# Attention: where the split of the queries stands, who clears the value tiles, and when the first weights are loaded

## The chip, the core and the metric

The kernel runs on one core of a Trainium2 chip as one program. The core has five engines, each with a queue of its own that runs in order: TensorE (PE in the rows) for matrix products, VectorE (DVE), ScalarE (ACT), GpSimd (POOL), and SyncE (SP), which here only issues DMAs. They wait for each other through semaphores. The metric is the time of the whole program on the device, in microseconds; lower is better.

## The reference

Three stages follow each other. Only the first is touched by the change.

```python
# attention: q, k, v are (2, 12, 448, 64), float32
scores = (1.0 / np.sqrt(64)) * np.matmul(q, k.transpose(0, 1, 3, 2))
scores = np.where(np.triu(np.ones((448, 448), dtype=bool), k=1), -1e9, scores)
scores = scores - np.max(scores, axis=-1, keepdims=True)
attn = np.exp(scores)
attn = attn / (np.sum(attn, axis=-1, keepdims=True) + 1e-09)
x = np.matmul(attn, v)                  # to (896, 768)
# feed-forward: w_in (768, 2048), w_out (2048, 768)
h = np.maximum(x @ w_in, 0.0)
x = h * h @ w_out
# mixture of 8 experts: each token goes to the one of its largest logit,
# out[mask] = gate * (relu(x[mask] @ w1[e]) @ w2[e])
```

## The kernel before, in words

**Pairs.** The 24 heads are handled as 12 pairs of two heads (`units`, number 0 to 11), since two heads of 64 fill the 128 partitions. The 448 queries are cut into seven chunks of 64 (`c`, 0 to 6); chunk `c` meets only the first (c+1)*64 keys. One score product has on its rows 64 queries of one head and 64 of the other; the tile q2 holds the queries with zeros where the other head's rows would be, so that one product serves both heads.

**Splits.** Float32 numbers are handled as a rounded part and the rest, so that a product of two of them is three products of rounded numbers: kh with the rounded queries, kl with them, kh with the queries' rest. `s_prep` makes these: the rounded keys `kh` (VectorE, line 62), their rest `kl` (GpSimd, line 67), the rounded and scaled queries (ScalarE, line 60) and their rest (VectorE, line 202). For pair 0 the query parts are written directly into q2, half the partitions at a time. For all other pairs they are written into a staging tile `qs`, and two DMAs copy them into q2 (line 216). There are two q2 tiles (names q_109 and q_110 in the order), two `kh` and two `kl`, for pairs in turn; the zeros in q2 are written once, at the start, by GpSimd.

**One pair's way.** Scores (TensorE, line 243) in the order of chunks 2, 0, 1, 3, 6, 4, 5, into one of four PSUM tiles; the row maximum (VectorE, line 253; for pair 0 a plain reduction, line 250); the exponential with its sum (ScalarE, line 256); one over the sums (`rs`, lines 264 and 265); the normalisation (GpSimd, line 269); transposes of the probabilities (TensorE, line 287) into one of two PSUM tiles; their split (ScalarE line 60, VectorE line 67, `pt`); the product with the values (line 305), whose tiles `v` are split in the same way (`s_prep_v`) and have a middle third of zeros; and the split of the result into xhi and xlo.

**Order.** The loop over `k` (line 427) records half a pair at a time: with even `k`, chunks 6, 4, 5 of pair k/2 + 1; with odd `k`, chunks 2, 0, 1, 3 of the pair behind it, with transposes and value products of earlier pairs between them. TensorE keeps the recorded order up to `k` = 21 (`man_a`), and GpSimd keeps it in the start only (`zeros`). Everywhere else a scheduler orders the instructions of each engine by its own model, subject to data, buffers and explicit pins: `tc.issue_after(x)` keeps an instruction behind instruction x. In `s_prep` of pair u + 3 both the key rounding and the query split are pinned behind the maximum and the exponential of chunk 5 of the pair two before it. A small `V.memset` on one column (`hold`) ties a load to a place in VectorE's queue.

**Weights.** `w_load` brings one 128-row slice of w_in (768 KB of raw 8-byte words), which VectorE assembles into float32 (lines 121 to 125) and GpSimd splits. Loads of slice `f` are pinned behind the query copies of pair 6 + f; there are two raw buffers, and the conversions are pinned near the end of attention. The feed-forward products (`phase_a`) follow attention on TensorE, mixed into its last pairs.

## Time and profile before

| what | value |
|---|---|
| median of three runs | 561.88 us (560.63 to 562.13) |
| the profiled execution, its own time | 561.91 us |
| its span, first to last instruction | 560.2 us |
| mean granted TensorE clock | 0.996 of full speed |
| TensorE busy | 541.2 us (97%) |
| VectorE, ScalarE, GpSimd busy | 397.6, 288.3, 183.4 us |
| TensorE's waits, 57.5 to 98.5 us | 1.8 for copies of q, 0.4 for exponentials, 0.2 for pt |

All rows come from one execution. Attention fills roughly the first 100 us of the span. In rows of a timeline the first number is the start and the second the length of the group, both in us; then the engine, the line of the kernel, the operation, what it writes and reads, shape and count; in brackets stands the idle time of the engine just before, with what ended it. Idle time of an engine that nobody waits for costs nothing. TensorE's products overlap in the pipeline, so the lengths of neighbours add up to more than the time between their starts.

### The profile page before, as it was taken

What the parts mean: (1) busy time and instruction counts of PE and PEld (TensorE: products, weight loads), DVE (VectorE), ACT (ScalarE), POOL (GpSimd) and SP (SyncE); (2) the same over time, 40 slices, a digit from 0 to 9 for tenths busy, and PEclk for the clock granted to TensorE, in tenths of its full rate; (3) what the DMA queues carried; (4) which work ended last, traced back from release to release, by engine and by line L of the source; (5) the groups of instructions that cost most, each with busy time, mean ns of one, the idle gap of its engine ahead of it and who ended that gap; (6) DMA issues with size and microseconds to landing.
All of it is one profiled execution on the core that took longest, in us unless ns stands there. A gap on an engine that the chain in (4) does not pass through costs nothing.

```text
span 560.2 us, 9639 instructions
## 1 busy us (share of the span) xinstructions
PE 541.2 (97%) x3429; PEld 504.4 (90%) x3430; DVE 397.6 (71%) x957; ACT 288.3 (51%) x638; POOL 183.4 (33%) x229
## 2 busy tenths in 40 slices
PE   8899999999999999999999999999999999999993
PEld 5799889988999999999999989989999899999992
DVE  6888889755887977696653376896186898873641
ACT  4888778314425243424333236721286787763641
POOL 8878789926645643221000001001201301300010
PEclk9999999999999999999999999999999999999998
DMA  6657653332545555361000008503958879874310
GB/s 205 176 121 206 210 137 99 126 103 67 170 137 201 168 170 180 113 217 56 1 30 28 1 28 337 215 14 88 375 171 268 305 243 360 293 231 160 109 53 6
DMA packets 28234, 86.52 MB, mean 154 GB/s; under 512 B 2822, under 2 KB 13062, under 8 KB 28176
## 3 DMA queue, kind: packets, MB, share of 16 engines
q1 hardware_dynamic: 26640, 79.51, 44.0%
q0 software_dynamic: 1536, 6.29, 3.1%
q8 instruction: 29, 0.48, 0.3%
q14 instruction: 29, 0.24, 0.1%
HBM read 75.24 MB, written 6.29 MB: 146 GB/s over the span
## 4 chain that ended last, share of the span: by engine, by line
PE 83%; DVE 6%; ACT 4%; DMA 3%; issue 2%; POOL 1%; SPq 0%; POOLq 0%; ACTq 0%; DVEq 0%
PE yps L607 20%; PE ops L977 9%; PE pa L329 7%; PE pa L331 7%; PE pa L330 7%; PE pv L305 5%; PE s L243 4%; PE hps L878 3%; PE ops L915 3%; PE pt L287 2%; PE ops L910 2%; PE hps L896 2%; PE hps L898 2%; PE hps L897 2%; DVE ml L67 2%
## 5 line engine op out<-in xcount | busy, mean ns | idle before, releaser
L67 DVE TENSOR_TENSOR ml<-xraw,mh 128x768 fp32r<-128x768 f32 x64 | 59.7, 957 | 10.3 <-ACT mh L60 9.8
L60 ACT ACTIVATE mh<-xraw 128x768 fp32r<-128x768 f32 x64 | 52.3, 843 | 7.6 <-PE ops L910 5.8
L977 PE MATMUL ops<-mh,act 128*128 128x384 f32 x224 | 53.5, 342 | 0.0
L243 PE MATMUL s<-kh,q 128*128 128x128 f32 (+6 forms) x168 | 45.7, 318 | 3.8 <-ACT p L256 2.0
L256 ACT ACTIVATE p<-s,mn 128x192 f32<-128x192 f32 (+6 forms) x84 | 39.6, 478 | 16.5 <-DVE mn L253 11.5
L305 PE MATMUL pv<-pt,v 128*128 128x448 f32 (+7 forms) x288 | 47.0, 297 | 0.7 <-ACT pt L60 0.6
L269 POOL TENSOR_SCALAR p<-p,rs 128x192 f32<-128x192 f32 (+6 forms) x84 | 44.9, 552 | 4.9 <-DVE rs L265 4.5
L1003 POOL DMA_INDIRECT out<-osb,fsi x10 | 10.9, 1088 | 97.3 <-ACT osb L998 65.9
L125 DVE SCALAR_TENSOR_TENSOR w<-raw,w 128x768 int32<-128x768 int32 x32 | 41.7, 1304 | 0.7
L305 PEld LDWEIGHTS pv<-pt,v 128*128 128x128 f32 (+1 forms) x288 | 38.2, 163 | 2.7 <-ACT pt L60 0.8
L977 PEld LDWEIGHTS ops<-mh,act 128*128 128x128 f32 x224 | 39.3, 188 | 0.8
L1015 POOL DMA_INDIRECT xr<-ydram,fgi x10 | 10.5, 1051 | 86.2 <-DVE fsi L723 45.4
L67 DVE TENSOR_TENSOR pt<-pt 128x512 fp32r<-128x512 f32 x48 | 31.9, 682 | 9.1 <-ACT pt L60 9.0
L243 PEld LDWEIGHTS s<-kh,q 128*128 128x128 f32 x168 | 31.9, 205 | 7.0 <-ACT p L256 5.5
L67 DVE TENSOR_TENSOR hs<-h,hs 128x512 fp32r<-128x512 f32 (+1 forms) x32 | 21.8, 690 | 22.9 <-ACT hs L60 22.7
L253 DVE CUSTOM_DVE_ANT_0 s<-s,maskf 128x192 f32<-128x192 f32 (+6 forms) x77 | 32.2, 432 | 8.2 <-PE s L243 5.9
L123 DVE SCALAR_TENSOR_TENSOR w<-raw,w 128x768 int32<-128x768 int32 x32 | 37.1, 1160 | 0.7
L67 DVE TENSOR_TENSOR ml<-mraw,mh 128x768 fp32r<-128x768 f32 x32 | 29.9, 956 | 10.2 <-ACT mh L60 9.8
L335 ACT ACTIVATE relu<-pa 128x448 f32<-128x448 f32 x32 | 17.0, 538 | 34.0 <-PE pa L331 34.0
L60 ACT ACTIVATE pt<-pt 128x512 fp32r<-128x512 f32 x48 | 28.3, 599 | 7.0 <-PE pt L287 6.8
L121 DVE TENSOR_SCALAR w<-raw 128x768 int32<-128x768 int32 x32 | 22.6, 705 | 12.4 <-POOL wi3l L67 3.2
L1015 POOL DMA_INDIRECT xr<-ydram,egi x2 | 2.3, 1149 | 84.0 <-DVE esi L723 83.7
(463 smaller groups left out, 1667.1 us busy)
## 6 DMA issues: line engine op xcount, KB each, us to landing
xraw<-in_wm SPq DMA_DIRECT2D x32, 768.0 KB, 5.4
raw<-in_w_in SPq DMA_DIRECT2D x16, 768.0 KB, 4.2
raw<-in_w_out SPq DMA_DIRECT2D x16, 768.0 KB, 4.3
mraw<-in_wm SPq DMA_DIRECT2D x16, 768.0 KB, 5.0
qk<-in_qkd SPq DMA_DIRECT2D x11, 448.0 KB, 5.0
q<-qs SPq DMA_DIRECT2D x22, 224.0 KB, 3.8
v<-in_vd SPq DMA_DIRECT2D x12, 256.0 KB, 3.0
ydram<-ysb SPq DMA_DIRECT2D x7, 384.0 KB, 2.3
```

The costliest lines, as they stand in the source:

```text
L60: return A.activation(out, in_, AF.Copy, scale=scale)
L67: return eng.tensor_tensor(out=lo, in0=x, in1=hi, op=ALU.subtract)
L125: V.scalar_tensor_tensor(out=w[:, x], in0=raw[:, x, 0], scalar=29, in1=w[:, x], op0=ALU.logical_shift_right, op1=ALU.bitwise_or)
L243: T.matmul(ss, d["q2"][:, c, :, :, x].rearrange("p a b -> p (a b)"), d[y][:, :n], start=i_ == 0, stop=i_ == 2 and not first)
L256: last["exp", units.index(u), c] = A.activation(d["p"][c][:, :n], ss, AF.Exp, bias=mn, scale=1.0 if first else -1.0, accum_out=d["sm"][:, ...
L269: last["norm"] = G.tensor_scalar(out=p, in0=p, scalar1=rs[:, COL[c]:COL[c] + 1], scalar2=1.0, op0=ALU.mult, op1=ALU.mult)
L305: T.matmul(d["pv"][:, j * P:S] if h else d["pv"][0:D, j * P:S], d[x][:, j, 1:3].rearrange("p a b -> p (a b)") if h else d[x][:, j, 0], pt[ ...
L329: T.matmul(ps, wh[:, c], xhi[:, kc, gs], start=(kc == 0), stop=False)
L330: T.matmul(ps, wh[:, c], xlo[:, kc, gs], start=False, stop=False)
L331: T.matmul(ps, wl[:, c], xhi[:, kc, gs], start=False, stop=(kc == KC - 1))
L607: T.matmul(ps[t][c][:, :384], x, w[:, c * 384:(c + 1) * 384], start=(f == 0 and w is wh and x is hi), stop=(f == NF - 1 and x is lo))
L977: T.matmul(ps[c], x, ww[:, c * 384:(c + 1) * 384], start=(fc == 0 and x is hh and ww is wh), stop=(fc == 7 and x is hl))
```

## The change

Six things are altered, all in attention. (1) `qdir` goes from 1 to 2: pair 1's queries, as pair 0's, are split directly into q2, without `qs` and without copies. Its `s_prep` is recorded after pair 0's first products, and its rest is pinned behind the maximum of pair 0's chunk 3. (2) From pair 2 on the pins are separate: the rounded query copy behind the exponential of chunk 6 (instead of chunk 5, which is two exponentials later), the rest of the queries behind the maximum of chunk 5, and the key rounding behind that rest. (3) The zeros of the four value tiles are written by ScalarE as copies of a tile of zeros (`zero_v`) instead of by GpSimd. (4) The table `tri` is made later, at `k` = 5. (5) The loads of pair 1's values and pair 3's queries are held behind pair 0's maximum of chunk 3. (6) Loads of w_in are pinned behind the copies of pair 9 + f.

```diff
-    ch=(((2, 0, 1), (3,), ()), ((6,), (4, 5), ())), wn=[3, 2, 2], qh="A", qdir=1, qss=2, rpin=5, qdma="SS", kh="V",
+    ch=(((2, 0, 1), (3,), ()), ((6,), (4, 5), ())), wn=[3, 2, 2], qh="A", qdir=2, qss=2, rpin=5, qdma="SS", kh="V",
...
-        pin = last.get(("q", 6 + f)) if src is w_in else None
+        pin = last.get(("q", 9 + f)) if src is w_in else None
...
+    def zero_v(*xs):
+        for x in xs:
+            A.activation(x[:, :, 1], wz[:, 0:NB * D].rearrange("p (a b) -> p a b", b=D), AF.Copy)
...
-    def s_prep(u):
+    def s_prep(u, hi_pin=None, lo_pin=None, k_pin=None):
...
-        if i != 1:
+        if i == 0:
             round_k()
+            lo_pin = last["kh"]
...
-            copy_on(ENG[CFG["qh"]], hi, q, scale=SCALE)
-            return V.scalar_tensor_tensor(out=lo, in0=q, scalar=SCALE, in1=f32(hi), op0=ALU.mult, op1=ALU.subtract)
+            with behind(hi_pin):
+                last["hi"] = copy_on(ENG[CFG["qh"]], hi, q, scale=SCALE)
+            with behind(lo_pin):
+                last["lo"] = V.scalar_tensor_tensor(out=lo, in0=q, scalar=SCALE, in1=f32(hi), op0=ALU.mult,
+                                                    op1=ALU.subtract)
...
+        if i > 0:
+            with behind(last["lo"]), behind(k_pin):
+                round_k()
...
+    zero_v(*vz[0])
     s_prep(units[0])
+    with behind(last["hi"]):
+        zero_v(*vz[1])
...
-            with tc.issue_after(last["q"].ins):
-                load_v(units[1])
-                s_load(units[3])
+            load_v(units[1], last["max", 0, 3])
+            s_load(units[3], last["max", 0, 3])
...
-        if k == -3:
-            s_prep(units[1])
-            for x in vz[0] + vz[1]:
-                G.memset(f32(x[:, :, 1]), 0.0)
-            zero_p(1)
-            G.memset(tri, 1.0)
...
+        if k == -3:
+            s_prep(units[1], None, last["max", 0, 3])
+            zero_p(1)
+            zeros.__exit__(None, None, None)
...
-            x = (0, 3) if u < 0 else (u + 1, 5)
-            with tc.issue_after(last["max", *x].ins), tc.issue_after(last["exp", *x].ins):
-                s_prep(units[u + 3])
+            i = u + 1
+            s_prep(units[u + 3], last["exp", i, 6 if i else 3], last["max", i, 5 if i else 6], last["max", i, 5])
```

The first place is VectorE at the start, from the rest of pair 0's second head on. `mn` are the row maxima of pair 0, `rs` the sums before and after the reciprocal, `qs` and q_110 the query rests of pairs 1 and 2, `kh` the rounded keys. Before:

```order
L202 SCALAR_TENSOR_TENSOR q_109<-qk,q_109 64x7x64
L202 SCALAR_TENSOR_TENSOR qs<-qk,qs 128x448
L62 CAST kh<-qk 128x448
L250 TENSOR_REDUCE mn<-s 128x1 x4
L264 TENSOR_SCALAR rs<-sm 128x4
L265 RECIPROCAL rs<-rs 128x4
L202 SCALAR_TENSOR_TENSOR qs<-qk,qs 128x448
L250 TENSOR_REDUCE mn<-s 128x1 x2
L62 CAST kh<-qk 128x448
L250 TENSOR_REDUCE mn<-s 128x1
```

And now, in the changed kernel's line numbers:

```order
L215 SCALAR_TENSOR_TENSOR q_109<-qk,q_109 64x7x64
L263 TENSOR_REDUCE mn<-s 128x1 x4
L215 SCALAR_TENSOR_TENSOR q_110<-qk,q_110 64x7x64 x2
L62 CAST kh<-qk 128x448
L173 MEMSET v 128x1
L173 MEMSET qk 128x1
L277 TENSOR_SCALAR rs<-sm 128x4
L278 RECIPROCAL rs<-rs 128x4
L263 TENSOR_REDUCE mn<-s 128x1
L215 SCALAR_TENSOR_TENSOR qs<-qk,qs 128x448
L263 TENSOR_REDUCE mn<-s 128x1 x2
L62 CAST kh<-qk 128x448
```

The first four maxima have moved ahead of pair 1's split and key rounding, the split is two half-height instructions, and the fifth maximum stands ahead of pair 2's split instead of behind it.

The second place is the preparation of pair 6, behind the scores of pair 4: on ScalarE the query copy (`qs`) among the exponentials of chunks 6, 4 and 5 (128x448, 128x320, 128x384), before and then now:

```order
L256 ACTIVATE p_121,sm<-s,mn 128x448
L256 ACTIVATE p_119,sm<-s,mn 128x320
L60 ACTIVATE pt<-pt 128x512
L256 ACTIVATE p_120,sm<-s,mn 128x384
L60 ACTIVATE qs<-qk 128x448
```

```order
L269 ACTIVATE p_121,sm<-s,mn 128x448
L60 ACTIVATE qs<-qk 128x448
L269 ACTIVATE p_119,sm<-s,mn 128x320
L60 ACTIVATE pt<-pt 128x512
L269 ACTIVATE p_120,sm<-s,mn 128x384
```

The copy has moved ahead of two exponentials and one copy of transposed probabilities. On VectorE at the same place, from the maximum of chunk 5 on, before and then now (`ISA` is the masked maximum, two rows each):

```order
L253 ISA s,mn<-s,maskf 128x384
L253 ISA mn 128x1
L62 CAST kh<-qk 128x448
L265 RECIPROCAL rs<-rs 128x4
L253 ISA s,mn<-s,maskf 128x192
L253 ISA mn 128x1
L67 TENSOR_TENSOR pt<-pt 128x512
L253 ISA s,mn<-s,maskf 128x64
L253 ISA mn 128x1
L253 ISA s,mn<-s,maskf 128x128
L253 ISA mn 128x1
L202 SCALAR_TENSOR_TENSOR qs<-qk,qs 128x448
```

```order
L266 ISA s,mn<-s,maskf 128x384
L266 ISA mn 128x1
L215 SCALAR_TENSOR_TENSOR qs<-qk,qs 128x448
L62 CAST kh<-qk 128x448
L67 TENSOR_TENSOR pt<-pt 128x512
L266 ISA s,mn<-s,maskf 128x192
L266 ISA mn 128x1
```

The split of the queries has moved ahead of the key rounding, three maxima and one subtraction; the key rounding has moved back by one instruction.

The third place is SyncE's queue, where the first two loads of w_in stand among the query copies (`q`), queries and keys (`qk`) and values (`v`). Before, from the copies of pair 6 on, and now, from those of pair 9 on:

```order
L216 DMA q_109<-qs 64x7x128 x2
L176 DMA qk<-in_qkd 128x896
L116 DMA raw<-in_w_in 128x1536
L183 DMA v<-in_vd 128x512
L216 DMA q_110<-qs 64x7x128 x2
L176 DMA qk<-in_qkd 128x896
L116 DMA raw<-in_w_in 128x1536
```

```order
L226 DMA q_110<-qs 64x7x128 x2
L183 DMA qk<-in_qkd 128x896
L116 DMA raw<-in_w_in 128x1536
L226 DMA q_109<-qs 64x7x128 x2
L190 DMA v<-in_vd 128x512
L116 DMA raw<-in_w_in 128x1536
```

Both loads stand three pairs later.

## Rows read from the trace of the kernel before

**Rows 1.** Timeline of TensorE: the first score product of pairs 5 to 11.

```profile
43.16 0.34 PE L243 MATMUL s<-kh,q 128*128 128x192 f32 x1
...
50.72 0.34 PE L243 MATMUL s<-kh,q 128*128 128x192 f32 x1
...
59.62 0.34 PE L243 MATMUL s<-kh,q 128*128 128x192 f32 x1 [1.09 <-DMA q<-qs]
...
67.53 0.34 PE L243 MATMUL s<-kh,q 128*128 128x192 f32 x1
...
76.00 0.33 PE L243 MATMUL s<-kh,q 128*128 128x192 f32 x1 [0.67 <-DMA q<-qs]
...
83.81 0.34 PE L243 MATMUL s<-kh,q 128*128 128x192 f32 x1
...
92.03 0.33 PE L243 MATMUL s<-kh,q 128*128 128x192 f32 x1 [0.42 <-ACT p L256]
```

**Rows 2.** The chain of waits, at its longest DMA: start, us, what.

```profile
70.49 5.38 DMA q<-qs
```

**Rows 3.** Timeline of SyncE's queue: copies of pair 7, second weight load.

```profile
53.37 1.28 SPq L216 DMA_DIRECT2D q<-qs  x2
...
55.57 1.08 SPq L116 DMA_DIRECT2D raw<-in_w_in  x1
```

**Rows 4.** Timelines of VectorE and ScalarE around the preparation of pair 11.

```profile
83.50 0.39 DVE L62 CAST kh<-qk 128x448 fp32r<-128x448 f32 x1
...
85.36 0.71 DVE L202 SCALAR_TENSOR_TENSOR qs<-qk,qs 128x448 fp32r<-128x448 f32 x1
...
83.16 0.53 ACT L256 ACTIVATE p<-s,mn 128x320 f32<-128x320 f32 x1 [1.15 <-DVE mn L253]
...
84.70 0.62 ACT L60 ACTIVATE qs<-qk 128x448 fp32r<-128x448 f32 x1
```

**Rows 5.** Timeline of VectorE in the start.

```profile
7.82 1.17 DVE L250 TENSOR_REDUCE mn<-s 128x1 f32<-128x192 f32 x4
9.85 1.57 DVE L264 TENSOR_SCALAR rs<-sm 128x4 f32<-128x4 f32 x1 [0.86 <-ACT p L256]
...
12.07 0.62 DVE L250 TENSOR_REDUCE mn<-s 128x1 f32<-128x448 f32 x1
...
18.95 1.18 DVE L62 CAST kh<-qk 128x448 fp32r<-128x448 f32 x1
```

**Rows 6.** Timeline of GpSimd in the start.

```profile
4.54 1.38 POOL L67 TENSOR_TENSOR kl<-qk,kh 128x448 fp32r<-128x448 f32 x1 [0.60 <-DVE kh L62]
...
8.77 1.13 POOL L67 TENSOR_TENSOR kl<-qk,kh 128x448 fp32r<-128x448 f32 x1
9.84 1.07 POOL L453 MEMSET v<- 128x256 f32 x4
10.85 0.41 POOL L154 MEMSET p<- 128x64 f32 x4
...
18.60 1.28 POOL L67 TENSOR_TENSOR v<-v,v 128x512 fp32r<-128x512 f32 x1
```

**Rows 7.** Line 202, the query split: duration in ns, min/median/max, starts.

```profile
L202 DVE SCALAR_TENSOR_TENSOR qs<-qk,qs x11: 597/626/712, 7.0 to 85.4; 128x448 fp32r<-128x448 f32 x11
L202 DVE SCALAR_TENSOR_TENSOR q<-qk,q x2: 610/1012/1415, 4.3 to 5.0; 64x448 fp32r<-64x448 f32 x2
```

**Rows 8.** Timeline of ScalarE: the first query copy.

```profile
3.45 1.23 ACT L60 ACTIVATE q<-qk 64x448 fp32r<-64x448 f32 x2 [1.16 <-DMA qk<-in_qkd]
```

**Rows 9.** TensorE's waits, 98.5 to 131 us: us in total, times, longest.

```profile
PE pv L305 <- ACT pt L60: 0.6, 1, 0.6
...
PE pv L305 <- DVE pt L67: 0.2, 1, 0.2
```

**Rows 10.** Timeline of GpSimd: rounding of the first weights.

```profile
98.46 0.82 POOL L62 CAST wi0h<-w 128x768 fp32r<-128x768 f32 x1
```

**Rows 11.** The page's costliest groups: the normalisation, busy us, mean ns.

```profile
L269 POOL TENSOR_SCALAR p<-p,rs 128x192 f32<-128x192 f32 (+6 forms) x84 | 44.9, 552 | 4.9 <-DVE rs L265 4.5
```

More of the change, by code (lines that the diff above doesn't have):

```diff
@@ L1 @@
 import numpy as np
-from contextlib import ExitStack
+from contextlib import ExitStack, nullcontext
 import concourse.bass as bass
@@ L146, in build @@
     tri = cpool.tile([P, P], BF16, name="tri")
+    wz = apool.tile([P, 512], BF16, name="wz")
+    V.memset(wz, 0.0)
     def zero_q(i):
@@ L160, in ab, with hold, s_load @@
         return ENG[x[units.index(u) % len(x)]]
-    def hold(x, behind):
-        if behind is not None:
-            with tc.issue_after(behind.ins):
+    def hold(x, late):
+        if late is not None:
+            with tc.issue_after(late.ins):
                 V.memset(x, 0.0)
-    def s_load(u, behind=None):
+    def s_load(u, late=None):
         b, pr = u
         qk = apool.tile([P, 2, S], F32, tag="qk", bufs=CFG["qkraw"], name="qk")
-        hold(qk[:, 0, 0:1], behind)
+        hold(qk[:, 0, 0:1], late)
         if u == units[0]:
@@ L177, in s_load, with load_v, behind @@
         st[u] = dict(q=qk[:, 0], k=qk[:, 1])
-    def load_v(u, behind=None):
+    def load_v(u, late=None):
         b, pr = u
         st[u]["v"] = v = apool.tile([P, NB, P], F32, tag="v", bufs=CFG["vraw"], name="v")
-        hold(v[:, 0, 0:1], behind)
+        hold(v[:, 0, 0:1], late)
         last["load"] = last["load", units.index(u)] = DMA.dma_start(out=v, in_=vd[b, pr])
-    def s_prep(u):
+    def behind(ins):
+        return nullcontext() if ins is None else tc.issue_after(ins.ins)
+    def s_prep(u, hi_pin=None, lo_pin=None, k_pin=None):
         d = st[u]
@@ L194, in round_k @@
             last["kh"] = copy_on(ab("kh", u), d["kh"], d["k"])
-        if i != 1:
+        if i == 0:
             round_k()
+            lo_pin = last["kh"]
         def split(r, hi, lo):
             q = d["q"][r].rearrange("p (c a) -> p c a", a=QC)
-            copy_on(ENG[CFG["qh"]], hi, q, scale=SCALE)
-            return V.scalar_tensor_tensor(out=lo, in0=q, scalar=SCALE, in1=f32(hi), op0=ALU.mult, op1=ALU.subtract)
+            with behind(hi_pin):
[3 more added lines that the diff above has]
+                                                    op1=ALU.subtract)
         heads = [slice(h * D, (h + 1) * D) for h in range(2)]
         if i < CFG["qdir"]:
-            with tc.issue_after(last["kh"].ins):
-                for h, r in enumerate(heads):
-                    split(r, d["q2"][r, :, h, :, 0], d["q2"][r, :, h, :, 1])
+            for h, r in enumerate(heads):
+                split(r, d["q2"][r, :, h, :, 0], d["q2"][r, :, h, :, 1])
         else:
             q = apool.tile([P, NQ, QC, 2], F32R, tag="qs", bufs=CFG["qss"], name="qs")
-            lo = split(slice(0, P), q[:, :, :, 0], q[:, :, :, 1])
-            if i == 1:
-                with tc.issue_after(lo.ins):
-                    round_k()
+            split(slice(0, P), q[:, :, :, 0], q[:, :, :, 1])
             for h, r in enumerate(heads):
                 last["q"] = last["q", i] = ENG[CFG["qdma"][h]].dma_start(out=f32(d["q2"][r, :, h]), in_=f32(q[r]))
+        if i > 0:
+            with behind(last["lo"]), behind(k_pin):
+                round_k()
         lo_of(ab("kl", u), d["kl"], d["k"], f32(d["kh"]))
@@ L365, in build @@
     zero_q(1)
-    wz = apool.tile([P, 512], BF16, name="wz")
-    V.memset(wz, 0.0)
     wp = ps_v.tile([P, 512], F32, tag="pv", name="wp")
@@ L429, in build @@
         if k == -2:
-            with tc.issue_after(last["q"].ins):
-                load_v(units[1])
-                s_load(units[3])
+            load_v(units[1], last["max", 0, 3])
+            s_load(units[3], last["max", 0, 3])
         elif h == 0:
             if u + 4 < NU:
-                with tc.issue_after(last["q"].ins):
+                with behind(last["q"]):
                     s_load(units[u + 4])
@@ L449, in build @@
             man_a.__exit__(None, None, None)
-        if k == -3:
-            s_prep(units[1])
-            for x in vz[0] + vz[1]:
-                G.memset(f32(x[:, :, 1]), 0.0)
-            zero_p(1)
-            G.memset(tri, 1.0)
-            G.affine_select(out=tri, in_=tri, pattern=[[1, P]], compare_op=ALU.is_gt, fill=0.0, base=0,
-                            channel_multiplier=-1)
-            zeros.__exit__(None, None, None)
         norm_at(k)
         products(k, half_unit(k))
+        if k == -3:
+            s_prep(units[1], None, last["max", 0, 3])
+            zero_p(1)
+            zeros.__exit__(None, None, None)
+        if k == 5:
+            with behind(last["norm"]):
+                G.memset(tri, 1.0)
+                G.affine_select(out=tri, in_=tri, pattern=[[1, P]], compare_op=ALU.is_gt, fill=0.0, base=0,
+                                channel_multiplier=-1)
         if k + 3 < len(CFG["wn"]):
```

## The prediction

> **What bounds the kernel now.** I read the busy table first: TensorE is busy for nearly the whole span, so a change in attention counts only where TensorE stands still, and every stall taken from it should arrive at the end. The second view is TensorE's timeline, read at one fixed mark, the first score product of a pair (128x192, kh). Between 43.16 and 50.72 us one pair takes 7.56 us with no idle time marked [rows 1]. That is the length to which all later marks are compared. From 50.72 on they stand 8.90, 7.91, 8.47, 7.81 and 8.22 us apart [rows 1]: 1.34, 0.35, 0.91, 0.25 and 0.66 us too long, 3.51 together. The two longest excesses begin with idle time of 1.09 and 0.67 us, and both name the DMA that copies the split queries from `qs` into the zero-padded tile q2; the last one names an exponential (0.42).
>
> The third view is the chain of waits and the SyncE queue. The chain holds 5.38 us of that DMA at 70.49, landing at 75.87, just before TensorE's 76.00 [rows 2]. For the first stall, the copies were issued from 53.37 on and a weight load of 768 KB followed at 55.57 [rows 3]; TensorE got its queries at 59.62. So the copy is late because it starts late, with a slow landing on top.
>
> The fourth view, VectorE and ScalarE inside one pair, shows why it starts late. After the pair's last maximum VectorE first rounds the keys (83.50) and does the rest of the query split only at 85.36; ScalarE's rounded copy of the queries stands at 84.70, behind an exponential at 83.16 before which ScalarE had been idle for 1.15 us [rows 4]. The fifth view is the start, up to 21 us, on VectorE and GpSimd [rows 5 to 7], where VectorE sits between TensorE's scores and ScalarE's exponentials.
>
> **The change part by part.**
>
> *Query copies two exponentials sooner, rests ahead of the key rounding.* Nothing is added; per pair one ScalarE and one VectorE instruction move. The split comes to where the key rounding began: 85.36 - 83.50 = 1.86 us sooner [rows 4]. ScalarE's copy now stands ahead of the exponential at 83.16, inside the 1.15 us in which that engine was idle, and needs about 0.62 [rows 4], so it is ready when VectorE comes. The copy DMAs follow the split on SyncE and move by the same 1.86. The second stall's landing moves from 75.87 to 74.01, while TensorE wants it at 76.00 - 0.67 = 75.33 [rows 1, 2]: 1.3 us to spare. In the first, TensorE wanted it at 58.53 and had it at 59.62 at the latest; 1.86 sooner is 57.76, 0.77 to spare. Both stalls go: -(1.34 + 0.91) = -2.25 us. Of the 0.35 and 0.25 in the pairs behind them, while the other engines fall back into step, I take half: -0.30 (ends: 0 and -0.60). The 0.66 at the last mark is an exponential's and stays. What is late next: key rounding and its GpSimd rest move 0.6 us back, as does VectorE's subtraction on the transposed probabilities. The keys have most of a period. The subtraction frees one of two PSUM tiles; I cost it at nothing in the steady part, since the same split stood two or three instructions later in the same queue and the sum up to the third maximum is unchanged. If that cover fails it costs 0.6 a pair (see the rivals).
>
> *Weights later.* The first two 768 KB loads go behind the copies of pairs 9 and 10 instead of 6 and 7. Before, these raw bytes wait long for VectorE anyway, whose conversion falls at the end of attention; no cost. The gain is that no weight load runs beside pair 7's copy; it is already in the 2.25, since the earlier start alone clears that stall. What may replace it: the loads now run beside pairs 10 and 11, with 0.8 to 1.3 us to spare.
>
> *Second pair split in place.* Two copy DMAs of pair 1 vanish; ScalarE and VectorE do two half-height instructions each instead of one: 0.61 us each on VectorE when unblocked [rows 7]. These and the key rounding now stand behind the first four maxima, which end at 7.82 + 1.17 = 8.99 [rows 5]. So: 8.99 + 1.22 + 0.39 for the rounding [rows 4] + 0.1 for two one-column clears (estimate) = 10.7, where the scaling sum `rs` can start.
>
> *Zeros.* Before, `rs` starts at 9.85 and takes 1.57 us, ending at 11.42, as GpSimd's run of clears ends (four from 9.84, four until 11.26 and that of `tri` behind them) [rows 5, 6]. Four of these, 1.07 us, leave GpSimd, and `tri` too; they go to ScalarE, which is idle for 1.16 us ahead of the first query copy [rows 8] and longer ahead of the second. A zero copy has 256 columns; from below a quarter of a 448-column one, from above one whole (0.62, [rows 4]): two take 0.3 to 1.24, I take 0.9, and at most 0.1 us shows.
>
> *Start, summed.* With `rs` at 10.7 and unblocked, the fifth maximum starts at about 11.0 instead of 12.07 [rows 5]: 1.05 sooner. But pair 2's split follows it, and GpSimd's subtraction on pair 1's keys starts only now, at about 10.75, since the keys were rounded late. Beside the same subtraction at 4.54 a split took 1.415 instead of 0.610 [rows 6, 7]. So the split ends near 12.6, and the sixth maximum starts there; before, it started at 12.07 + 0.62 = 12.69. The gain shrinks to 0.1. Later, at 18.95, the key rounding waits 1.18 us until GpSimd's value subtraction (18.60 + 1.28) is done [rows 5, 6]. Now the split stands there and waits as long, with the rounding behind it, so that the probabilities' subtraction comes 0.6 later, in a stretch where TensorE waits for it. I take +0.4 for that, hence +0.3 for the whole start. Ends: -1.05 (no blocking) and +1.2 (`rs` starts after GpSimd, below, plus the whole 0.6).
>
> *Handover to the feed-forward part.* From 98.5 to 131 TensorE's order is remade; its three waits there, the longest 0.6 and two of 0.2 us [rows 9], show that at most 1.0 can be won. On GpSimd the rounding of the first weights, 0.82 us [rows 10], moves ahead of three normalisations of pair 10: at most 0.8 lost. I take 0.
>
> Behind 131 us nothing moves, and TensorE sets the pace. Sum: -2.25 - 0.30 + 0.3 + 0 = -2.25 us, from the profiled execution's own 561.91 to 559.7. That execution lies within 0.1 us of the median of the three runs (561.88), so no correction.
>
> **A rule weighed against these rows.** In the rows, splits that run beside GpSimd's normalisations, which read SBUF as well, take 597 to 712 ns in all eleven cases [rows 7]: no block. Only GpSimd's two-input subtractions and runs of clears hold VectorE up. The Trainium skill (SBUF — State Buffer, section "Who interferes with whom") says that a VectorE instruction with two SBUF inputs and a GpSimd instruction that reads SBUF block each other fully, the later one waiting. For subtractions the trace agrees; for normalisations it does not, and the measurement decides. By the rule the nine moved splits could each wait out one normalisation, 552 ns on average [rows 11], 5.0 us on VectorE; the sum here takes none of it.
>
> **The rivals.**
>
> A. The forecast, 559.7.
>
> B. The start wins as well: GpSimd and VectorE do not meet, and the 1.05 stays, without the 0.4: 559.7 - 1.3 = 558.4. For it: GpSimd's queue is four clears, 1.07 us, shorter there [rows 6]. Against: the key subtraction falls exactly on the split.
>
> C. The start gives back. `rs` and the key subtraction become ready within 0.1 us of each other. If GpSimd wins, `rs` waits until subtraction and four clears are over, 10.75 + 1.13 + 0.41 = 12.3 [rows 6], and the fifth maximum comes 0.55 later than before; with the 0.6 at 18.95 that is +1.2 in place of +0.3: 560.6.
>
> D. The copies stay late, since weight loads now meet pairs 10 and 11: the idle times (1.76) return there: 561.5. For it: a landing took 5.38 us even without a weight load beside it.
>
> E. Slower. The split and the key rounding, 1.0 us in one block, stand ahead of the subtraction that frees a PSUM tile for the next transposes. It decides if that tile has under 0.6 us to spare in an unstalled pair; then TensorE waits 0.6 in each of nine pairs, 5.6 us against 2.25: 565.3. For it: TensorE does wait for that subtraction in the start. Against: after it, between 43.16 and 50.72, there is no such wait though VectorE does the same work.
>
> **How the numbers follow.** A 0.48, B 0.17, C 0.18, D 0.10, E 0.07. About 0.3% (1.7 us) is what a measurement of this kernel tells from no change: 560.2 is the border. A lies under it but for a fifth of its spread (0.10), B under, C and D inside, E above: faster 0.55, same 0.38, slower 0.07. The range from 557.9 (B with the handover's gain in part) to 561.7 (D) leaves out E and the edges, 2 in 10.
>
> **What would show it.** Right: no idle time of TensorE put down to the copy DMA anywhere; marks 7.6 us apart from the fourth pair to the last; copies issued about 1.9 us nearer to the last maximum; the mark at 43.16 within 1 us of where it stood. C shows as a long `rs` or a long split before 13 us; E as TensorE waiting for VectorE's subtraction in pair after pair; D as copy waits after 70 us. The forecast is wrong if the marks stay 8 us or more apart, or if TensorE idles more than 1 us between 95 and 130.

## The result and the profile after

The changed kernel takes 556.92 us (median of 5 runs, 556.48 to 557.33) against 561.88 us of the kernel before beside it (560.63 to 563.17): a ratio of 0.9912, 95% interval 0.9894 to 0.9931, 4.96 us less. That is under the forecast's range (559.7, 557.9 to 561.7) and 2.7 us more gain than its sum of 2.25. The profiled execution of the changed kernel took 557.04 us, its span is 555.3 against 560.2. Timed twice more, beside other kernels, the changed kernel took 556.93 and 556.92 us, with the kernel before at 561.35 and 561.41.

The page of the kernel after, in its busy row and its group of score products (out<-in, count, busy us and mean ns, idle time before them and what ended it):

```profile
PE 539.0 (97%) x3429; PEld 502.5 (90%) x3430; DVE 398.5 (72%) x960; ACT 291.0 (52%) x643; POOL 183.4 (33%) x225
L256 PE MATMUL s<-kh,q 128*128 128x128 f32 (+6 forms) x168 | 44.5, 311 | 0.7 <-ACT p L269 0.7
```

The score products had 3.8 us of idle time ahead of them before the change; 0.7 is left, all of it in the start. TensorE's timeline at the marks of [rows 1], pairs counted from 0 as there:

```profile
41.07 0.34 PE L256 MATMUL s<-kh,q 128*128 128x192 f32 x1
...
48.63 0.34 PE L256 MATMUL s<-kh,q 128*128 128x192 f32 x1
...
56.19 0.34 PE L256 MATMUL s<-kh,q 128*128 128x192 f32 x1
...
71.36 0.34 PE L256 MATMUL s<-kh,q 128*128 128x192 f32 x1
...
86.47 0.34 PE L256 MATMUL s<-kh,q 128*128 128x192 f32 x1
```

No idle time stands at any of them, and the steps are 7.56 us (one is 7.61). From pair 5 to pair 11 the way is 45.40 us where it was 48.87 in [rows 1]; pair 5 itself comes 2.09 us earlier. SyncE's queue, which answers to [rows 3], and VectorE and ScalarE around the preparation of pair 11, which answer to [rows 4]:

```profile
49.00 1.27 SPq L226 DMA_DIRECT2D q<-qs  x2
...
64.21 1.28 SPq L226 DMA_DIRECT2D q<-qs  x2
...
66.43 1.00 SPq L116 DMA_DIRECT2D raw<-in_w_in  x1
```

```profile
78.21 0.60 DVE L266 CUSTOM_DVE_ANT_0 s<-s,maskf 128x384 f32<-128x384 f32 x1
...
78.91 0.63 DVE L215 SCALAR_TENSOR_TENSOR qs<-qk,qs 128x448 fp32r<-128x448 f32 x1
79.46 0.39 DVE L62 CAST kh<-qk 128x448 fp32r<-128x448 f32 x1
...
77.63 0.66 ACT L60 ACTIVATE qs<-qk 128x448 fp32r<-128x448 f32 x1
78.45 0.53 ACT L269 ACTIVATE p<-s,mn 128x320 f32<-128x320 f32 x1 [0.16 <-POOL v L67]
```

ScalarE's copy stands two exponentials sooner, ahead of the 320-column one, which waits 0.16 where it waited 1.15. The split stands right behind the last maximum. Pair 7's copies are issued at 49.00, 7.19 us ahead of TensorE's product; in [rows 1, 3] they were issued 6.25 us ahead of one that had waited 1.09 for them, so the copies gained 2.0 us on the point where they are wanted (forecast: 1.86).

The start on VectorE, which answers to [rows 5]:

```profile
6.96 1.03 DVE L263 TENSOR_REDUCE mn<-s 128x1 f32<-128x192 f32 x4 [0.50 <-PE s L262]
8.03 1.25 DVE L215 SCALAR_TENSOR_TENSOR q<-qk,q 64x448 fp32r<-64x448 f32 x2
...
9.62 0.17 DVE L277 TENSOR_SCALAR rs<-sm 128x4 f32<-128x4 f32 x1
...
9.92 0.59 DVE L263 TENSOR_REDUCE mn<-s 128x1 f32<-128x448 f32 x1
10.43 1.02 DVE L215 SCALAR_TENSOR_TENSOR qs<-qk,qs 128x448 fp32r<-128x448 f32 x1
...
17.46 0.62 DVE L215 SCALAR_TENSOR_TENSOR qs<-qk,qs 128x448 fp32r<-128x448 f32 x1
18.00 0.38 DVE L62 CAST kh<-qk 128x448 fp32r<-128x448 f32 x1
```

The row sum `rs` takes 0.17 us in place of 1.57, so it won the race that rival C gave to GpSimd; pair 2's split meets GpSimd's key subtraction and takes 1.02 (forecast 1.4); and at 17.46 to 18.38 nothing is blocked, where 1.18 us of blocking was expected. The first four maxima start 0.86 us earlier than in [rows 5]. Two things allow it: pair 1's split and key rounding no longer stand ahead of them on VectorE, and TensorE finished the first pair's scores sooner, though nothing ahead of them was changed on TensorE. What the second is, *The clock in the start* below takes up.

### The profile page after: what moved, and what is told of

Its sections match the earlier page's. It is cut to its first block, busy times and chain, and to the rows that moved or that the text cites. A ratio compares the mean times of both kernels' runs of the same rounds, so it can differ in the third digit from the quotient of the medians.

```text
span 555.3 us, 9625 instructions
## 1 busy us (share of the span) xinstructions
PE 539.0 (97%) x3429; PEld 502.5 (90%) x3430; DVE 398.5 (72%) x960; ACT 291.0 (52%) x643; POOL 183.4 (33%) x225
## 4 chain that ended last, share of the span: by engine, by line
PE 89%; DVE 5%; ACT 2%; DMA 1%; issue 1%; POOL 1%; POOLq 0%; DVEq 0%
PE yps L618 20%; PE ops L988 9%; PE pa L342 7%; PE pa L343 7%; PE pa L344 7%; PE pv L318 7%; PE s L256 5%; PE pt L300 4%; PE hps L889 3%; PE ops L926 3%; PE ops L921 2%; PE hps L907 2%; PE hps L909 2%; PE hps L908 2%; DVE ml L67 2%; PE hps L890 1%
## 5 line engine op out<-in xcount | busy, mean ns | idle before, releaser
L67 DVE TENSOR_TENSOR ml<-xraw,mh 128x768 fp32r<-128x768 f32 x64 | 59.7, 956 | 10.3 <-ACT mh L60 9.5
L256 PE MATMUL s<-kh,q 128*128 128x128 f32 (+6 forms) x168 | 44.5, 311 | 0.7 <-ACT p L269 0.7
L1014 POOL DMA_INDIRECT out<-osb,fsi x10 | 10.9, 1094 | 98.2 <-ACT osb L1009 65.8
L67 DVE TENSOR_TENSOR ml<-mraw,mh 128x768 fp32r<-128x768 f32 x32 | 29.9, 955 | 10.3 <-ACT mh L60 9.6
```

Of the source, the lines that this page charges most:

```text
L67: return eng.tensor_tensor(out=lo, in0=x, in1=hi, op=ALU.subtract)
L256: T.matmul(ss, d["q2"][:, c, :, :, x].rearrange("p a b -> p (a b)"), d[y][:, :n], start=i_ == 0, stop=i_ == 2 and not first)
```

## The experiments

Marks are the starts of a pair's first 128x192 kh product, as in [rows 1]. Pairs count from 0. Some texts on record count from one, those with "pair 4 on", "pairs 2 to 5", "pair 2" and "pair 3": "pair 4 on" is pairs 3 to 11 here.

**The two halves: steady part alone, start alone.** The kernel before with the new order and late weights (`steady_only`), its core:

```diff
-            with tc.issue_after(last["max", *x].ins), tc.issue_after(last["exp", *x].ins):
-                s_prep(units[u + 3])
+            if u >= 0:
+                s_prep(units[u + 3], last["exp", u + 1, 6], last["max", u + 1, 5], last["max", u + 1, 5])
+            else:
+                ...  # as before
-        pin = last.get(("q", 6 + f)) if src is w_in else None
+        pin = last.get(("q", 9 + f)) if src is w_in else None
```

> The kernel before, with only the steady part changed: pairs 4 to 12 get the earlier query copies and the rests ahead of the key rounding, and the weight loads go behind copies 9 and 10. The start (second pair through copies, value zeros and the triangle on GpSimd) is that of before. Order theory (the start's 2.1 us come from the order of VectorE and GpSimd there): the mark of pair 5 stays within 0.3 us of 43.16, the marks behind it stand 7.56 apart, and the whole gain is what the steady part gave in the changed kernel, 3.5 us less what the handover takes back (0.66): 558.4 to 559.1. Clock theory (TensorE's products become short at a moment of the start that differs from run to run, whatever the order): the mark of pair 5 may stand near 41 here too. The forecast's own terms: 559.4.

The changed kernel with exactly these two put back (`start_only`):

```diff
-        pin = last.get(("q", 9 + f)) if src is w_in else None
+        pin = last.get(("q", 6 + f)) if src is w_in else None
...
+            if i:
+                with tc.issue_after(last["max", i, 5].ins), tc.issue_after(last["exp", i, 5].ins):
+                    s_prep(units[u + 3], old=True)   # key rounding, then the split
+            else:
+                ...  # as in the changed kernel
```

> The changed kernel with the steady part put back: from pair 4 on key rounding, query copy and split stand behind the sixth score tile's maximum and exponential again, and the weight loads go behind copies 6 and 7. Order theory: the mark of pair 5 stands near 41.1, the copy waits come back in pairs 7 and 9, 559.8 (gain 2.1, and the steady 3.5 lost, less the 0.66 of the handover if that belongs to it: 559.1 to 559.8). Clock theory: the mark of pair 5 falls anywhere from 41 to 43.2, and so does the moment from which the 128x192 products take under 0.2 us apiece. The forecast's terms: 562.2 (start +0.3).

Measured: steady part alone 558.08 us (557.63 to 558.36), ratio 0.9928 [0.9904, 0.9951]; start alone 560.64 (558.93 to 562.22), 0.9971 [0.9954, 0.9988], beside 561.93 of the kernel before. So the steady part alone is worth 3.85 us, 1.3 more than the forecast's 2.55, and the start alone 1.3, where 0.3 was to be lost. How far the two add up is settled to about 1 us only. Their sum of 5.1 is about the whole by the changed kernel's 556.92, which was timed apart from them. But `weights6` (below), the changed kernel but for the place of the weights, was timed beside them and took 557.83: 4.1 us for both together, 2.8 for the new order where the start is in, and 0.25 for the start where the new order is in. The same kernel took 556.41 when it was timed again, so steps under about 1.4 us between kernels that were not timed together are not safe.

The mark of pair 5 stood at 42.16 with the steady part alone (43.16 was expected: pair 3's copies are no longer waited for), and at 42.68 with the start alone (41.1 was expected). There TensorE waited 0.71 us for pair 3's copies and its clock read 0.50 from 14 to 16 us; the copies of pairs 8, 9 and 11 were waited for as well.

Where the 1.3 of the steady part comes from stands in the trace of the kernel before. There TensorE waits at the first score product of four pairs from pair 3 on, not of two. Two of these waits the profile puts down to an exponential: the 0.42 in [rows 1] and this one, which lies ahead of the stretch that the prediction read:

```profile
28.05 0.34 PE L243 MATMUL s<-kh,q 128*128 128x192 f32 x1 [0.91 <-ACT p L256]
```

In the run of the steady part alone the same product starts before the exponential that was named has begun (TensorE, then ScalarE):

```profile
27.03 0.34 PE L246 MATMUL s<-kh,q 128*128 128x192 f32 x1
...
27.36 0.57 ACT L259 ACTIVATE p<-s,mn 128x384 f32<-128x384 f32 x1
```

So that exponential is no condition of the product. Its queries are. The copies of pairs 3, 7, 9 and 11 in the kernel before, two to a row (ns, first and last start), with the time from issue to landing under each; pair 5's copies last, for comparison:

```profile
L216 SPq DMA_DIRECT2D q<-qs x2: 602/612/623, 22.1 to 22.8; - x2
DMA to landing us min/median/max: 3.3/4.3/5.2
...
L216 SPq DMA_DIRECT2D q<-qs x2: 602/613/624, 53.4 to 54.0; - x2
DMA to landing us min/median/max: 5.0/5.2/5.5
...
L216 SPq DMA_DIRECT2D q<-qs x2: 602/612/622, 69.8 to 70.5; - x2
DMA to landing us min/median/max: 3.3/4.4/5.4
...
L216 SPq DMA_DIRECT2D q<-qs x2: 597/607/617, 86.1 to 86.8; - x2
DMA to landing us min/median/max: 3.7/4.4/5.2
...
L216 SPq DMA_DIRECT2D q<-qs x2: 602/612/622, 38.2 to 38.8; - x2
DMA to landing us min/median/max: 3.3/3.6/3.8
```

Second issue plus longest landing gives about 28.0, 59.5, 75.9 and 92.0 us; TensorE's waits end at 28.05, 59.62, 76.00 and 92.03. All four are copies, the two named after exponentials too. Nor is it the issue that sets these pairs apart. Pair 5's copies were issued 5.0 us ahead of its product (38.2, 43.16) and were in time; those of the four pairs were issued 5.0 to 5.5 us ahead of the moment at which TensorE wanted them (pair 7: 53.37, 58.53). Their longest landing took 5.2 to 5.5 us, pair 5's 3.8.

**Which of the two steady edits.** The changed kernel with the weights put back behind copies 6 and 7 (twice), and with the order put back but the weights late:

```diff
-        pin = last.get(("q", 9 + f)) if src is w_in else None
+        pin = last.get(("q", 6 + f)) if src is w_in else None     # weights6, weights6_again
```

> The changed kernel with the first weight loads behind copies 6 and 7 again, all else as changed. The forecast's reading (the earlier start of the copy alone clears the stall): no wait for a copy, time within 0.3 us of 557.0. Rival (the weight load beside pair 7's copy makes it slow): TensorE waits 0.3 to 1.1 us for the copy in pair 7, 557.3 to 558.0.

> The changed kernel with the weight loads behind copies 6 and 7, once more. Landing theory and forecast: the earlier issue leaves 1.0 us and more to spare even for a landing of 5.5, no copy wait, within 0.4 us of the changed kernel's time in this call. Rival: 0.9 us slower as in the first run (557.83), with a copy wait in pair 7 or 8.

> The changed kernel with the old order from pair 4 on (key rounding, then query copy and split behind the sixth score tile's maximum and exponential), but the weight loads still behind copies 9 and 10. Landing theory (a copy's second half lands 5.0 to 5.5 us after its issue in some pairs, and only the earlier issue hides that): waits for copies come back in two to four pairs, named after the copy or after an exponential, 560.0 to 560.6, no better than the run that also put the weights back (560.64). Weights theory (the loads beside pairs 7 and 8 were what made the copies late): 557.5 to 558.5.

> The changed kernel, unchanged, beside the two others on the same chip: 556.9, marks 7.56 us apart from pair 4 on, no wait for a copy.

Measured: weights back 557.83 (556.56 to 558.81) and then 556.41 (556.06 to 557.56), the changed kernel beside the second 556.92 (555.96 to 557.36), no copy wait in any of the three traces. The first run's 0.9 us did not come again; moving the weights is worth nothing that can be told here. The old order with late weights: 559.14 (558.11 to 561.80), ratio 0.9964 [0.9945, 0.9983], 2.2 us over the changed kernel beside it, with waits in three pairs. The first of them was named after an exponential once more, and its copies landed late once more (TensorE, then SyncE's copies of that pair):

```profile
45.01 0.34 PE L257 MATMUL s<-kh,q 128*128 128x192 f32 x1 [0.97 <-ACT p L270]
```

```profile
L227 SPq DMA_DIRECT2D q<-qs x2: 602/612/622, 38.8 to 39.5; - x2
DMA to landing us min/median/max: 4.9/5.2/5.4
```

The profiled execution was the slowest of its runs (561.80; its granted clock also fell to 0.50 from 24 to 27 us), so it shows the kind of wait and not the median's number of them. Its median lies between the two expectations (560.0 and more, 558.5 and less), and its interval overlaps that of the run with both edits undone; the order is the larger part for certain, and all of it within the spread.

**The two parts of the start.** The changed kernel with the value zeros back on GpSimd (`zeros_g`), and with the second pair through copies, ahead of the first maxima (`qdir1`):

```diff
-    zero_v(*vz[0])
-    with behind(last["hi"]):
-        zero_v(*vz[1])
+            for x in vz[0] + vz[1]:                       # zeros_g: behind s_prep(units[1])
+                G.memset(f32(x[:, :, 1]), 0.0)
```

```diff
-    qdir=2
+    qdir=1
-            s_prep(units[1], None, last["max", 0, 3])     # behind the first products
+            s_prep(units[1])                              # qdir1: ahead of them, as before
```

> The changed kernel with the four value zeros back on GpSimd, behind the second pair's key subtraction, and none on ScalarE. Order theory: GpSimd's run of clears again stands beside VectorE's first row sum or the third pair's split, which takes 1.5 us or more, and the marks from pair 2 on come 0.5 to 1.1 us later: 557.5 to 558.1. Clock theory: no change beyond the moment at which the products become short, 557.0.

> The changed kernel with the second pair's queries split through qs and copies again, ahead of the first maxima as before; value zeros on ScalarE, triangle late, steady part as changed. With the run whose zeros were back on GpSimd and the run with the steady part alone this makes a square of the start's two parts. Order theory: the first row sum rs takes about 0.2 instead of 1.57 us, since the four clears that held it are gone, which gives 0.5 to 1.1 of the start's 1.2 us: 557.0 to 557.6. Rival (the split in place is what matters, since it takes 0.62 + 0.39 us out of VectorE's way ahead of the first four maxima): 558.0. Clock theory: the products become short at about 6.5 or 9.9 us, whichever, and the time follows that.

Measured: zeros on GpSimd 557.71 (557.44 to 558.10), timed beside 558.08 of the steady part alone and 557.83 of `weights6`; copies for the second pair 556.86 (555.88 to 557.40), timed beside 556.93 of the changed kernel. The second says that the split in place is worth nothing that shows. What the start gains then lies in what `qdir1` keeps of it: the zeros on ScalarE, the late `tri` and the held loads. Of these the traces point at the zeros; the times do not show it, since `zeros_g` is as fast as `weights6` beside it. The row sum in `qdir1` (`rs`, the four sums plus 1e-9), on VectorE, behind the same split through `qs` as in [rows 5], and the key rounding that races GpSimd's value subtraction; then GpSimd beside the row sum:

```profile
9.74 0.43 DVE L277 TENSOR_SCALAR rs<-sm 128x4 f32<-128x4 f32 x1 [1.01 <-ACT p L269]
...
10.30 0.59 DVE L263 TENSOR_REDUCE mn<-s 128x1 f32<-128x448 f32 x1
...
18.02 1.47 DVE L62 CAST kh<-qk 128x448 fp32r<-128x448 f32 x1
```

```profile
9.74 0.41 POOL L161 MEMSET p<- 128x64 f32 x4
```

0.43 us against 1.57, from nearly the same start, with four clears on GpSimd beside it instead of four larger ones, these four and that of `tri`. In both traces the sum ends within 0.03 us of the last clear (10.15 here, 11.39 in the kernel before): that block was GpSimd's run of clears. In the three other traces with before's start it took 1.58, 1.58 and 1.59. In `zeros_g` the sum was not held (0.17), nor was a split held longer than in the changed kernel, as its expectation had it; there GpSimd's normalisations start at 12.23 behind the clears, in place of 11.29, and the mark of pair 5 stands at 41.67, 0.6 to 0.7 us later than in the changed kernel. The rounding at 18.02 does lose 1.08 us to the subtraction, as the forecast had it, and TensorE then waits 1.70 us for the probabilities; yet the mark of pair 3 stands at 25.93 against 25.95 of the changed kernel, which shows 0.76 and 0.38 there. The 0.4 that the sum took for this was not to be seen at the end.

**The clock in the start.** The kernel before, the steady part alone and the changed kernel once more, unchanged:

> The kernel before once more, for a second look. Two questions. First, the copies: in the first look four idle times of TensorE (0.91, 1.09, 0.67, 0.42 us) end 0.05 to 0.12 us after the second copy of pairs 3, 7, 9 and 11 lands, 5.2 to 5.5 us after its issue; the copies of the other pairs land after 3.2 to 3.8. If that landing is what sets the wait, slow landings will again coincide with waits, perhaps at other pairs, and the time follows their number (558.7 to 563.8 in the timed runs). Second, the products of the first pair: if they become short at about 6.3 us here too, the moment differs from run to run; if at 9.9 again, it belongs to this start.

> The kernel before with the steady part alone changed, once more, for a second look at the start of before. Clock theory (differs from run to run): products short from 5 to 7 us, mark of pair 2 near 10.9 instead of 12.19, time 557.2 to 558.4. If the late moment belongs to this start: short from 9.9 again, 12.2, 558.1.

> The changed kernel once more, unchanged, to compare the others of this call with and for a second look at its start. Order theory: the marks of pairs 2 to 5 within 0.3 us of the first look (10.48, 17.62, 25.95, 33.51). Clock theory (the moment at which TensorE's products become short differs from run to run): s<-kl of the first pair may take 0.30 us apiece until 9.9, as in the kernel before, and the marks may move by up to 1.8 us. Time 557.0.

The four kl products of pair 0 and the three warm-up products behind the first scores, in the kernel before, first execution and second (`before_again`), and from the second also VectorE ahead of the first maxima:

```profile
5.97 1.22 PE L243 MATMUL s<-kl,q 128*128 128x192 f32 x4
...
8.34 1.47 PE L374 MATMUL wp<-wz 128*128 128x512 bf16 x3
```

```profile
5.95 0.75 PE L243 MATMUL s<-kl,q 128*128 128x192 f32 x4 [0.46 <-POOL kl L67]
...
7.29 0.81 PE L374 MATMUL wp<-wz 128*128 128x512 bf16 x3
...
12.31 0.33 PE L243 MATMUL s<-kh,q 128*128 128x192 f32 x1 [0.94 <-DMA q<-qs]
...
13.52 0.30 PE L243 MATMUL s<-kh,q 128*128 128x64 f32 x1 [0.63 <-ACT p L256]
```

```profile
7.52 0.39 DVE L62 CAST kh<-qk 128x448 fp32r<-128x448 f32 x1
7.82 1.01 DVE L250 TENSOR_REDUCE mn<-s 128x1 f32<-128x192 f32 x4
```

The times were 562.60 us (the kernel before, one run), 558.34 (the steady part alone, one run) and 556.93 (the changed kernel, 556.04 to 557.81); in `before_again` the same four pairs waited for their copies. One kernel, TensorE at work from 1.39 us on in both, and products at the lower level (1.2 GHz, 1.47 us for three of 512 columns) until 9.9 us in one execution, at the upper one (2.4 GHz, 0.81) before 6 in the other. Of 17 traces of all kernels the rise came late in 5 and by about 6.5 us in 12; the first trace of before was a late one and that of the changed kernel an early one.

An early rise alone moves nothing in before's start. Its first four maxima start at 7.82 in both executions, behind pair 1's split and key rounding on VectorE, and its pair 1 stands at 12.26 and, early, at 12.31, where it waits for its copies; in the second trace of the steady part, early too, it stands at 12.09, where the clock theory wanted 10.9. The 0.86 us by which the changed kernel's maxima came sooner and the 1.8 us of its pair 1 (10.48) thus took both, the changed start and an early rise.

What an early rise is worth further on depends on the start too. In both early traces of before's start TensorE gains nothing: it waits 0.94 us (0.89 in the other) for the second pair's copies and then 0.63 (0.70) for an exponential, and from about 14 us on its clock is down again. `qdir1`, early, waits 0.96 for its copies but not for that exponential; its clock stays up and its pair 5 stands at 41.06. One stretch of `before_again` and of the changed kernel's second trace, by engine, granted clock (PEclk) third from the end:

```profile
16.00:17.00 1.00, 1.00 (x3) 0.87 (x3) 0.71 (x3) 0.70 (x4) 1.00 (x2) 0.50 0.90 257
```

```profile
16.00:17.00 1.00, 0.76 (x5) 0.37 (x4) 1.00 (x4) 1.00 (x4) 1.00 (x3) 1.00 0.94 295
```

The clock reads 0.50 somewhere behind 13 us in six of the 17 traces: `before_again`, `steady_again`, `weights6`, `start_only`, `q1_vlate` and `old_order`. The mark of pair 5 with before's start and the new steady part, late and then early, both 558.3 us in all; and with the changed start made late by the kernel that follows:

```profile
42.16 0.34 PE L246 MATMUL s<-kh,q 128*128 128x192 f32 x1
...
42.78 0.34 PE L246 MATMUL s<-kh,q 128*128 128x192 f32 x1
...
41.97 0.34 PE L256 MATMUL s<-kh,q 128*128 128x192 f32 x1
```

With the changed start and an early rise it stood at 41.07, 40.97, 41.01 and 41.01 in four traces, and at 41.51 in a fifth, `weights6`, in which the clock fell. The kernel that makes the rise late:

```diff
-    warm=8
+    warm=4
```

> The changed kernel with 4 warm-up products of 128x512 ahead of the first scores instead of 8; TensorE then idles from about 3.2 us to its first score product at 4.8. Clock theory: the products stay long (0.30 us for the 128x192 ones) until 9.9 us or later, the first four maxima come 0.9 us later, and if the clock is what the start's gain rests on, the mark of pair 5 stands 0.8 to 1.2 us later, time 557.8 to 558.2. Order theory: VectorE's and GpSimd's order sets the marks and the mark of pair 5 moves under 0.4: 557.0 to 557.4.

Measured: 557.76 (557.06 to 558.14). TensorE idles 1.42 us ahead of its first score product, the rise comes at about 10.3 us, and the marks of pairs 1 and 5 stand at 12.18 and 41.97: pair 5 0.2 us better than before's start with a late rise, where the early traces are 1.3 to 1.8 apart. The forecast worked its start out from a late trace, and with a late rise VectorE's way came out close to it: the row sum at 10.54, the fifth maximum at 10.89, the sixth at 12.30 (10.7, 11.0 and 12.6 forecast). For such a start +0.3 against -0.2 is half a microsecond off; the medians hold both sorts in unknown shares. That the fall of the clock is what eats the early gain in before's start rests on two traces; no run forced it.

A third warm-up product behind the first pair's last scores, against the fall:

```diff
-    wn=[3, 2, 2]
+    wn=[3, 3, 2]
```

> The changed kernel with three warm-up products instead of two behind the first pair's last score tile, at about 10.2 us, where TensorE then waits for the second pair's keys. In two of the four looks at this start TensorE's products became long again from 13.4 to 16.6 us, and the mark of pair 3 stood 1.5 us later (19.17 against 17.62). If keeping TensorE busy there prevents it, no long products behind 10 us: 556.5 to 556.9. Rival: the product only pushes the second pair's scores back by 0.3: 557.0 to 557.3.

Measured: 557.48 (556.15 to 559.41 over 12 runs) beside 556.93. No fall in its trace, no gain in its time: inconclusive for the clock, since the unchanged start mostly shows none either.

**A version beyond the changed one.** Two of TensorE's waits left in its start are 0.76 and 0.38 us, at 19.64 and 21.63. Values of the second pair later on GpSimd, with either form of the start:

```diff
-                  tc.issue_after(last["norm", max(k - 2, -1)].ins)):
+                  tc.issue_after(last["norm", 0 if k == 1 else max(k - 2, -1)].ins)):
```

> The changed kernel with the value rounding of pair 2 (a cast and a subtraction on GpSimd, 0.61 and 1.27 us) held until GpSimd's normalisations of pair 2's first four tiles are issued, instead of those of pair 1. If TensorE's waits of 0.77 us at 19.6 and 0.38 at 21.6 rest on GpSimd's queue, in which the values stand ahead of the keys and of these normalisations, both go: 555.8 to 556.3. Rival: the value subtraction, now at about 24 us, holds VectorE's third key rounding or ScalarE's exponentials instead and nothing is gained: 556.9.

> The same late values, with the second pair's queries through copies ahead of the first maxima as in the kernel before (zeros on ScalarE). There VectorE's key rounding took 1.47 us at 18.0 beside GpSimd's value subtraction, and TensorE waited 1.70 at 20.6; with the values later the rounding should take 0.4 and the wait fall to 0.6 or less: 555.8 to 556.3, equal to the version with the split in place. If the split in place is worth something by itself, this one is 0.5 us or more slower than that.

Measured: 557.14 (555.93 to 558.63) and 557.52 (556.40 to 558.34), where 555.8 to 556.3 was expected. The two waits turned into 0.65 and 0.59 us for VectorE's subtraction on the probabilities, in both. Nothing gained; no kernel run here beats the changed one by more than its spread.

## Why the prediction was wrong

It had the mechanism of the larger part and missed its size; in the start it had the sign wrong.

- **"Both stalls go: -(1.34 + 0.91) = -2.25 us"**, and "the 0.66 at the last mark is an exponential's and stays": this is the step that failed first, by a term left out. There were four copy waits, not two. The wait of 0.66 was a copy's, and a fourth, at 28.05, lay ahead of the stretch that was read; against the run of the steady part alone it is worth 8.96 - 8.02 = 0.94 (the step from pair 2 to pair 3). With them the excess over 7.56 is 1.34 + 0.35 + 0.91 + 0.25 + 0.66 + 0.94 = 4.45; that run showed a 0.6 us longer step at pair 10 of its own, which leaves 3.85, as timed. These are single traces, so that it fits to the hundredth is luck. Adopting the releaser's name was the mistake: the marks of pairs 3 and 11 looked like those of 7 and 9 in everything but the label. And "late because it starts late, with a slow landing on top" put the two causes in the wrong order: the copies that stalled were issued as far ahead as pair 5's, which did not stall, and landed later. The wait left out at pair 3 is also 0.94 of the 2.09 us by which pair 5's mark moved, where under 1 was to show the forecast right.
- **The half of the "0.35 and 0.25"**: all of it went.
- **"Start, summed: +0.3"**: the start alone gave -1.3 beside the kernel before; where the new order is in, its gain is 0.25 by kernels timed together and 1.2 by kernels timed apart. The second term that failed. That `rs` would be freed was read rightly ([rows 5, 6], and the clears are its cause, as `qdir1` shows). Wrong were the two losses set against it: 0.4 for a blocked key rounding, which happened in `qdir1` (1.47 us) and cost nothing at the next mark; and a split of 1.41, which took 1.02. And the sum rested on one trace, with a late rise of the clock: in the traces with an early one the changed start reaches pair 5 1.3 to 1.8 us sooner than before's start, with a late one by 0.2. Rival B, "the start wins as well", at 0.17, had the sign right, but not the way: in it GpSimd and VectorE were not to meet, and they met at the split.
- **"Weights later: no cost", its gain already in the sum**: right, nothing measurable.
- **Zeros on ScalarE "at most 0.1 us shows"**: right on ScalarE (0.70 and 0.72 us for two, in idle time). What the move freed is GpSimd's side, where the clears had held `rs`.
- **The split in place** was costed as neutral to slightly bad with the rest; it is worth nothing that shows (556.86 without it, 556.93 with it).
- **"Handover 0"**: holds to within the spread. From pair 11's mark to the end the traces show 467.7 to 469.0 us, the three of the changed kernel alone 468.83, 468.83 and 467.87, the two of before 468.17 and 468.07.
- **The rule that was weighed**: by [rows 7] normalisations do not hold the split up. Of those eleven splits eight ran beside normalisations, not all eleven; the one at 6.98 ran beside a clear of 64x896 on GpSimd and took 0.63, so clears do not hold up everything on VectorE. The moved splits bore out the part on normalisations. The split's line in the changed kernel, ns min/median/max, and GpSimd's rows beside its slowest one (71.00, 1.30 us):

```profile
L215 DVE SCALAR_TENSOR_TENSOR qs<-qk,qs x10: 620/624/1302, 10.4 to 78.9; 128x448 fp32r<-128x448 f32 x10
...
70.53 1.28 POOL L67 TENSOR_TENSOR v<-v,v 128x512 fp32r<-128x512 f32 x1
71.79 2.11 POOL L282 TENSOR_SCALAR p<-p,rs 128x192 f32<-128x192 f32 x4
```

  The median is 624 against 626 in [rows 7]. Three splits of ten were slow (1.02 at 10.43, 0.98 at 55.88, 1.30 at 71.00), each beside a two-input subtraction of GpSimd (from 9.83, 55.09 and 70.53 on); the one at 78.91 ran 0.63 beside a normalisation from 79.01 on. The rule of the Trainium skill (SBUF — State Buffer, section "Who interferes with whom") agrees with the trace for subtractions and not for normalisations, and the marks 7.56 apart show that the 5 us it would have taken were not lost.
- Rivals C, D and E did not occur: `rs` took 0.17 us in every trace with the second pair split in place, and in the changed kernel no copy was waited for and no pair behind the start waited for VectorE's subtraction.

## What to carry to other kernels

A wait's releaser is a guess by time. When one consumer shows several waits at the same instruction of its loop, test the label against every one of them: add the issue time and the landing of each transfer, and look in another pair whether the engine named is a condition at all. Read the whole span for the pattern before pricing it, and take a second profile before a sum of half microseconds rests on the first ten: here the changed start had its pair 1 at 10.5 us or at 12.2, by the moment of the clock's rise. And compare kernels that were timed together: one kernel, timed twice, gave medians 1.4 us apart.

## What was not expected of the hardware

- From pair 3 on, copies of one size and queue landed after 3.2 to 4.2 us or after 4.8 to 5.5. In three traces with the old order (two of before, one of `old_order`) three or four pairs had the long sort, and TensorE's waits end with them; the fourth, `start_only`, has the waits, but the landings of those pairs are not in its trace. In the 13 traces with the new order no landing on record took over 4.1. So far as it is on record, the earlier issue did not have to cover a long landing: it met none. Why is open; which pairs had the long ones was the same in both traces of before and another in `old_order`.
- The moment at which TensorE's products become short is not set by the program: 1.22 or 0.75 us for the same four products of one kernel. The granted clock of the profile reads 1.00 in both (6 to 7 us); only the products' length tells them apart there, while at 16 us it shows the lower level as 0.50.
- A run of nine clears on GpSimd held a VectorE addition on 128x4 for 1.57 us, to the end of the run (1.57 to 1.59 in four traces); beside four small clears it took 0.43, and 0.17 with none beside it. What moving the clears to ScalarE is worth in the whole is not settled: between nothing and 1.2 us by the medians, by which runs are compared.
